# Moving tiles of the matmul pairs at one common word offset, 512 words apart, in a fused attention and relu² kernel

## The chip, the cores and the metric

The kernel runs on one core of one Trainium2 chip. The metric is the device time of one execution in microseconds (us). TensorE is called PE below, its weight loads PEld, VectorE DVE, ScalarE ACT, GpSimd POOL, and SyncE, which issues the transfers, SP. Memory on the core is counted in words of 4 bytes along one partition, and "phase" is used in this document for the first word of an operand modulo 64 words.

## The reference

Four batches of 12,480 tokens with 128 channels attend through 32 inducing points, and the result passes through a feed-forward layer with 2,048 hidden units, squared relu and an affine step.

```python
def mab(q, kv):
    s = scale * (q @ kv.transpose(0, 2, 1))
    s = s - s.max(-1, keepdims=True)
    a = np.exp(s)
    a /= a.sum(-1, keepdims=True) + 1e-09
    return a @ kv
h = mab(I, x)
x = mab(x, h)          # (B, N, C), then reshaped to (B * N, C)

h = x @ w_in
r = np.maximum(h, 0.0)
g = s * (r * r) + b
return (g @ w_out).astype(np.float32)
```

Inputs and output are float32; the two feed-forward weights come as 64-bit floats and are narrowed on the chip.

## The kernel before, in words

Tokens are worked on in 104 blocks of 480 (`BLK`), 26 for each batch. A block has 8 pairs (`NPAIR`), each of two chunks of 128 hidden units. For a pair, `pair` at L839 issues two matmuls at L850: weights from `wst` (the batch's inducing points already multiplied with `w_in`, in two float32r parts), moving operand the block's attention weights `a2t`, 128 partitions by 480 words. The result `h` goes through relu (`r`, on ACT at L865 or DVE at L867) and is squared twice: rounded to float32r as `g1` on ACT (`square`, L933), and in full as `g` on DVE (L888). Then `g2 = g - g1`, the small remainder, is made at L910, on POOL for 670 pairs and on DVE for 156. Finally `out_part` multiplies at L958 with w_out, six matmuls for each pair: `w_lo` and `w_hi` with both chunks of `g1`, and `w_hi` with both chunks of `g2`. So a pair costs eight float32r matmuls of 480 columns: two at L850, six at L958. The first six pairs (`NATIVE`) do without the remainder and multiply `g` in plain float32 with w_out.

Where these moving operands lie: `g1` is a tile of four chunks for two pairs (4 buffers), `g2` of two chunks for one pair (8 buffers), with chunks 480 words apart, and `a2t` one chunk (3 buffers, used in turn by the blocks). In the layout of the built program all `g1` and `g2` tiles begin at phase 48, so, since 480 is seven and a half times 64, their chunks alternate between phase 48 and 16. The three `a2t` buffers begin at phases 32, 0 and 32; blocks 2, 5, 8 and so on, counted from 0, have the one at phase 0. The weights `w_hi` and `w_lo` lie at phase 16, `wst` at phase 0.

The order on every engine is settled before the program is built: `Plan.run` simulates all engines with fixed durations (for example `MM` = 0.2174 us for each matmul), and the instructions are recorded in the order of that simulation. Each engine then runs its own list in order; semaphores hold it where an operand isn't ready. Before the first pair there is an opening of some 46 us in which batch 0's inducing points are computed (`p1_unit`, L429, `h_out`, L549, `attend_first`, L766), with the loads of x as the main traffic. The other batches' scores, values and attention weights (`scores`, `values`, `attend`) are spread between the pairs.

Small tiles that the change touches: `e` (the exponentials of the opening, two buffers, L459), the opening's `acc` (L434), `identr` (a float32r identity, used once at L804), and `t4` (a sum of parts of the identity, L229).

Of the kernel before, what the change touches and what calls it, by code (L numbers as in the profile page):

```python
# [10 lines left out]
F32 = mybir.dt.float32  # L11
F32R = mybir.dt.float32r
# [7 lines left out]
P = 128  # L20
T = 120
NQ = 4
BLK = T * NQ
# [40 lines left out]
    ("x", 5), ("w_in", 3), ("x", 6), ("w_out", 1), ("q", 5), ("w_out", 2), ("w_out", 3),  # L64
)
WARM = 6

# [84 lines left out]
def tile_attn_relu2(ctx: ExitStack, tc: tile.TileContext, xT, xN, xQ, indT, w_in, w_out, s_rep, b_rep, outT):  # L154
    nc = tc.nc
    B, _, N = xT.shape
    M = indT.shape[1]
# [5 lines left out]
    NG = -(-NBLK // GR)  # L163
# [3 lines left out]
    const = ctx.enter_context(tc.tile_pool(name="const", bufs=1))  # L167
    xt_pool = ctx.enter_context(tc.tile_pool(name="xt", bufs=XT))
    xn_pool = ctx.enter_context(tc.tile_pool(name="xn", bufs=4))
    p1 = ctx.enter_context(tc.tile_pool(name="p1", bufs=1))  # L170
    p2 = ctx.enter_context(tc.tile_pool(name="p2", bufs=2))
    wst_pool = ctx.enter_context(tc.tile_pool(name="wst", bufs=2))
    sm = ctx.enter_context(tc.tile_pool(name="sm", bufs=2))
    ew = ctx.enter_context(tc.tile_pool(name="ew", bufs=1))
# [37 lines left out]
    ind_sb = const.tile([P, M], F32, name="ind_sb")  # L212
    s_sb = const.tile([P, 1], F32, name="s_sb")
    b_sb = const.tile([P, 1], F32, name="b_sb")
    w_in_sb = const.tile([P, F], F32, name="w_in_sb")
    w_hi = const.tile([P, NF, P], F32R, name="w_hi")
    w_lo = const.tile([P, NF, P], F32R, name="w_lo")
    bias = const.tile([P, 1], F32, name="bias")
    ident = const.tile([P, P], F32, name="ident")
    make_identity(nc, ident)  # L220
    identr = const.tile([P, P], F32R, name="identr")
    nc.vector.tensor_copy(out=identr, in_=ident)
    ones = const.tile([P, M], F32, name="ones")
    nc.vector.memset(ones, 1.0)
# [1 line left out]
    nc.vector.memset(rebias, -896 * 2.0**23)  # L226

    sel = const.tile([P, P], F32, name="sel")
    t4 = sm.tile([P, 2, M], F32, name="t4", bufs=1)  # L229
    idv = ident.rearrange("p (r i) -> p r i", i=M)  # L230
    nc.vector.tensor_add(out=t4, in0=idv[:, 0:2, :], in1=idv[:, 2:4, :])
    nc.vector.tensor_add(
# [5 lines left out]
    def blocks_in(g):  # L238
        return min(GR, NBLK - g * GR)
# [188 lines left out]

    def p1_unit(g, ps, *waits):  # L429
        if not st:  # L430
            d = st[0] = {
                "mx": sm.tile([P, NG], F32, name="mx"),
                "l": sm.tile([P, NG], F32, name="l"),
                "acc": p1.tile([P, NG, P], F32, name="s"),  # L434
            }
            last = M * blocks_in(NG - 1)
            if last < P:
                nc.vector.memset(d["mx"][last:P, NG - 1:NG], -3.0e38)
                nc.vector.memset(d["l"][last:P, NG - 1:NG], 0.0)
                nc.vector.memset(d["acc"][last:P, NG - 1, :], 0.0)  # L440
        d = st[0]
        nb = blocks_in(g)
        rows = M * nb
        yield "PE", 0.98, ("x", 0, g, 1), *waits
        ps = ps()
        xt = xt_tiles[0, g, 1][0]
        for q in range(nb):
            nc.tensor.matmul(ps[M * q:M * (q + 1), 0:BLK], ind_sb, xt[:, q], start=True, stop=True)
        x_used(g, "s")
        yield "DVE", 0.69  # L450
        mx = d["mx"][0:rows, g:g + 1]
        nc.vector.reduce_max(out=mx, in_=ps[0:rows, 0:BLK], axis=AX.X)  # L452
        plan.set(("top", 0, g))
        yield "DVE", 0.08
        nm = sm.tile([P, 1], F32, name="nm")[0:rows]
        nc.vector.tensor_scalar_mul(nm, mx, -scale)
        e_turn, e_free = ring_in_order("e", 2)
        yield "ACT", 0.75, *e_free
        e = sm.tile([P, BLK], F32, name="e", bufs=2)  # L459
        plan.set(("e", "got", e_turn))  # L460
        nc.scalar.activation(
            out=e[0:rows], in_=ps[0:rows, 0:BLK], func=AF.Exp, bias=nm, scale=scale,
            accum_out=d["l"][0:rows, g:g + 1],
        )
        plan.set(("e", 0, g))
        yield "PE", 0.45
        for q in range(NQ):
            nc.tensor.transpose(ps[0:T, q * P:q * P + rows], e[0:rows, q * T:(q + 1) * T], ident[0:rows, 0:rows])
        plan.set(("e", e_turn))
        e_turn, e_free = ring_in_order("eT", 3)  # L470
        yield dict(ACT=0.49, DVE=0.61), 0.0, *e_free
        eT = sm.tile([T, NQ, P], F32, name="eT", bufs=3)
        plan.set(("eT", "got", e_turn))
        copy(eT[:, :, 0:rows], ps[0:T].rearrange("p (q i) -> p q i", q=NQ)[:, :, 0:rows])
        js = [g * GR // SB + h for h in range(-(-nb // SB))]
        yield "PE", 0.2 + 0.21 * nb, *[("turn", j) for j in js]
        for q in range(NQ):
            for n in range(nb):
                nc.tensor.matmul(  # L479
                    ps[M * n:M * (n + 1), 0:P], eT[:, q, M * n:M * (n + 1)],  # L480
                    home["xn"][js[n // SB] % 4][:, n % SB, q, :], start=(q == 0), stop=(q == NQ - 1),
                )
        plan.set(("eT", e_turn))
        for j in js:
            plan.set(("v done", j))
            if j >= NSB - 4:
                plan.set(("xn", j % 4))
        yield dict(ACT=0.18, DVE=0.21), 0.0
        copy(d["acc"][0:rows, g, :], ps[0:rows, 0:P])
        plan.set(("p1", 0, g))  # L490
# [227 lines left out]
    a2t, halves = {}, {}  # L718
# [47 lines left out]
    def attend_first(ps):  # L766

        yield "PE", 0.8, ("hT", 0), ("x", 0, 0, 2)
        ps = ps()
        xt = xt_tiles[0, 0, 2][0]  # L770
        for q in range(NQ):
            nc.tensor.matmul(
                ps[0:T, M * q:M * (q + 1)], xt[:, 0, q * T:(q + 1) * T], st[0]["hT"][:, 0:M], start=True, stop=True
            )
        v = ps[0:T, 0:P].rearrange("p (n i) -> p n i", i=M)
        sums = ps[0:T, P:P + NQ]
        yield "DVE", 0.28
        mx = sm.tile([P, TB], F32, name="mx2")[0:T, 0:NQ]
        nc.vector.reduce_max(out=mx, in_=v, axis=AX.X)
        yield "DVE", 0.28  # L780
        nc.vector.tensor_tensor(out=v, in0=v, in1=mx.unsqueeze(2).broadcast_to([T, NQ, M]), op=ALU.subtract)
        yield "ACT", 0.28
        nc.scalar.activation(out=v, in_=v, func=AF.Exp, scale=scale)
        yield "DVE", 0.28
        nc.vector.reduce_sum(out=sums, in_=v, axis=AX.X)
        yield "DVE", 0.16
        nc.vector.tensor_scalar_add(sums, sums, 1e-9)
        yield "DVE", 0.18
        l = sm.tile([P, TB], F32, name="l2")[0:T, 0:NQ]
        nc.vector.reciprocal(out=l, in_=sums)  # L790
        yield "DVE", 0.28
        nc.vector.tensor_tensor(out=v, in0=v, in1=l.unsqueeze(2).broadcast_to([T, NQ, M]), op=ALU.mult)
        yield dict(ACT=0.38, DVE=0.43), 0.0
        A = p2.tile([P, 2, WC], F32R, name="hl")
        A = A.rearrange("p a t -> p (a t)")[0:T, 0:NQ * P].rearrange("p (n r s i) -> p n r s i", n=NQ, r=2, s=2)
        vr = v.unsqueeze(2).broadcast_to([T, NQ, 2, M])
        copy(A[:, :, :, 0, :], vr)
        yield "DVE", 0.43
        nc.vector.tensor_tensor(out=A[:, :, :, 1, :], in0=vr, in1=A[:, :, :, 0, :].bitcast(F32), op=ALU.subtract)
        n, free = ring_in_order("a2t", 3)  # L800
        yield "PE", 0.5
        for q in range(NQ):
            w = A[:, q].rearrange("p r s i -> p (r s i)")
            nc.tensor.transpose(ps[:, q * T:(q + 1) * T].bitcast(F32R), w, identr[0:T, 0:T])  # L804
        yield dict(ACT=0.57, DVE=0.66), 0.0, *free
        t = p2.tile([P, BLK], F32R, name="a2t", bufs=3)
        plan.set(("a2t", "got", n))
        copy(t, ps[:, 0:BLK])
        a2t[0, 0] = t, n
        plan.set(("a2t", 0, 0))  # L810
        plan.set("first")

    def spread(b, g, q):

        turn, free = ring_in_order("a2t", 3)
        yield "SP", 2.4 if b or g else 1.6, *free, ("hl", b, g)
        t = p2.tile([P, BLK], F32R, name="a2t", bufs=3)
        plan.set(("a2t", "got", turn))
        hl, n, left = halves[b, g]
        for r in range(P // M):  # L820
            nc.sync.dma_start(
                out=t[M * r:M * (r + 1)].bitcast(F32), in_=hl[M * q:M * (q + 1), r % 2].bitcast(F32)
            )
        left.remove(q)
        if not left:
            plan.set(("hl", n))
        a2t[b, GR * g + q] = t, turn
        plan.events["a2t", b, GR * g + q] = landing(0.7) if b or g else landing(0.3, 1.7)
# [10 lines left out]
    def pair(k):  # L839

        b, blk, pr = place(k)
        n = pr % 2
# [5 lines left out]
        for u in range(2):  # L848
            c = 2 * pr + u
# [8 lines left out]
        q = quad[k - n]  # L858
# [4 lines left out]
        r = q["r_t"][:, half, :]  # L863
# [22 lines left out]
        g = hv if kind == "D" else ew.tile([P, 2, BLK], F32, name="g", bufs=4)  # L886
# [18 lines left out]
        n2, free2 = ring("g2", 8)  # L905
        yield ("Pool", 2.237, ("Q", k), free2) if kind == "P" else ("DVE", 1.065, C_U, ("Q", k), free2)
        hi = q["g1_t"][:, half, :]
        g2 = ew.tile([P, 2, BLK], F32R, name="g2", bufs=8)
        eng = nc.gpsimd if kind == "P" else nc.vector
        eng.tensor_tensor(out=g2, in0=g, in1=hi.bitcast(F32), op=ALU.subtract)  # L910
        plan.set(("h", turn) if kind == "D" else ("g", g_turn))
# [9 lines left out]
    def square(k0):  # L921

        q = quad[k0]
# [4 lines left out]
        if hi - lo == 2:  # L928
            plan.extend(0.8)
        if "g1_t" not in q:  # L930
            q["g1_t"] = ew.tile([P, 4, BLK], F32R, name="g1", bufs=4)
        sl = slice(2 * lo, 2 * hi)
        nc.scalar.activation(out=q["g1_t"][:, sl, :], in_=q["r_t"][:, sl, :], func=AF.Square)  # L933
        for i in range(lo, hi):
# [210 lines left out]
```

## Time and profile before

| | us |
|---|---|
| median of 3 runs | 1600.81 (1600.46 to 1603.71) |
| the profiled execution, device time | 1600.12 |
| its span from first to last instruction | 1598.0 |
| share of the span in which the chain that ended last stood on PE | 97% |

Durations of a trace come from the profiled execution, so sums are made against its 1598.0 us, and 2.1 us lie around the span. A matmul's end in the trace is modelled, and matmuls overlap in it: the distance from one start to the next, called the step below, is what a matmul costs. A row such as `x3304 | 1072.8, 380` gives the count, the busy time of all together, and the mean duration of one in ns.

### The profile page before, as it was taken

How to read it: one execution, taken by the hardware profiler on the slowest of the kernel's cores; microseconds unless marked ns; L12 is line 12 of the kernel's file. 1: busy time of each engine (PE TensorE's matmuls, PEld its weight loads, DVE VectorE, ACT ScalarE, POOL GpSimd, SP SyncE). 2: the span in 40 equal slices, each digit the busy share in tenths (PEclk: the TensorE clock that was granted, in tenths of full speed). 3: DMA queues.
4: the chain of work that ended last, by engine and by line, in shares of the span. 5: the costliest groups of instructions: out<-in, count | busy, mean ns of one | idle time of the engine just before them, and what ended most of it. 6: DMA issues, size and time to landing. Idle time of an engine off the chain costs nothing.

```text
span 1598.0 us, 24588 instructions
## 1 busy us (share of the span) xinstructions
PE 1584.9 (99%) x8155; PEld 1290.3 (81%) x8155; DVE 1485.2 (93%) x1603; ACT 1477.3 (92%) x1703; POOL 1499.6 (94%) x677
## 2 busy tenths in 40 slices
PE   8999999999999999999999999999999999999999
PEld 5578788888888778888788778888888888888887
DVE  6999899999999999999999899999999999999997
ACT  7799999999999989999999998999999999999997
POOL 0399999999999999999999999999999999999998
PEclk9999999999999999999999999999999999999999
DMA  8422323212223323211222322322221112112100
GB/s 292 125 92 89 128 77 107 81 32 89 75 75 112 99 100 112 84 59 57 82 68 88 118 76 91 120 79 63 84 56 61 38 50 69 32 50 69 57 27 24
DMA packets 54251, 131.17 MB, mean 82 GB/s; under 512 B 11518, under 2 KB 38014, under 8 KB 54126
## 3 DMA queue, kind: packets, MB, share of 16 engines
q1 hardware_dynamic: 54126, 129.61, 25.4%
q8 instruction: 66, 1.08, 0.3%
q14 instruction: 59, 0.48, 0.1%
HBM read 74.50 MB, written 25.56 MB: 63 GB/s over the span
## 4 chain that ended last, share of the span: by engine, by line
PE 97%; DMA 2%; DVE 1%; SPq 0%; ACT 0%; issue 0%; DVEq 0%; ACTq 0%
PE x L958 68%; PE h L850 24%; PE x L728 2%; PE x L676 1%; PE x L631 1%; DMA g<-in_w_in_dram 1%; DMA xn<-in_xQ_dram 0%; DMA xt<-in_xT_dram 0%; SPq L599 0%; PE x L581 0%; PE h L479 0%; DMA wst<-hl 0%; ACT xn L185 0%; DVE mx L452 0%; DVE wst L319 0%
## 5 line engine op out<-in xcount | busy, mean ns | idle before, releaser
L910 POOL TENSOR_TENSOR g<-g,g 128x960 fp32r<-128x960 f32 x670 | 1498.4, 2284 | 92.0 <-DVE g L888 75.4
L958 PE MATMUL x<-g,w_hi 128*128 128x480 f32 x3304 | 1072.8, 380 | 0.0
L933 ACT ACTIVATE g<-r 128x960 fp32r<-128x960 f32 (+1 forms) x766 | 803.5, 1072 | 33.7 <-DVE r L867 15.9
L888 DVE SCALAR_TENSOR_TENSOR g<-h,r 128x960 f32<-128x960 f32 x670 | 756.2, 1148 | 32.5 <-ACT r L865 23.1
L958 PEld LDWEIGHTS x<-g,w_hi 128*128 128x128 f32 x3304 | 620.3, 188 | 102.4 <-issue 3.9
L865 ACT ACTIVATE r<-h 128x960 f32<-128x960 f32 x639 | 613.2, 969 | 53.1 <-PE h L850 41.9
L958 PE MATMUL x<-g,w_lo 128*128 128x480 f32 x1652 | 628.0, 380 | 0.0
L850 PE MATMUL h<-a2t,wst 128*128 128x480 f32 x1664 | 510.3, 388 | 3.1 <-DMA wst<-hl 2.8
L850 PEld LDWEIGHTS h<-a2t,wst 128*128 128x128 f32 x1664 | 299.4, 188 | 103.0 <-issue 39.9
L958 PEld LDWEIGHTS x<-g,w_lo 128*128 128x128 f32 x1652 | 309.9, 188 | 52.2 <-issue 2.4
L867 DVE TENSOR_SCALAR r<-h 128x960 f32<-128x960 f32 x193 | 222.6, 1153 | 23.8 <-PE h L850 17.7
L888 DVE SCALAR_TENSOR_TENSOR h<-h,r 128x960 f32<-128x960 f32 x156 | 180.2, 1158 | 6.7 <-ACT r L865 6.1
L910 DVE TENSOR_TENSOR g<-h,g 128x960 fp32r<-128x960 f32 x156 | 179.2, 1151 | 4.7
L966 ACT ACTIVATE ob<-x,bias,s_sb 128x480 f32<-128x480 f32 x103 | 77.4, 752 | 12.8 <-PE x L958 12.3
L728 PE MATMUL x<-xt,hT 128*32 128x480 f32 x208 | 28.3, 578 | 0.0
L759 DVE TENSOR_TENSOR hl<-x,hl 128x480 fp32r<-128x480 f32 (+1 forms) x28 | 18.4, 657 | 9.8 <-ACT hl L185 9.7
L631 PE MATMUL x<-xt,ind_sb 128*32 128x480 f32 x156 | 21.2, 578 | 0.0
L734 DVE STREAM_TRANSPOSE x<-x 128x480 f32<-128x480 f32 (+1 forms) x28 | 19.3, 688 | 1.6 <-PE x L728 1.6
L676 PEld LDWEIGHTS x<-xn,eT 128*32 128x32 f32 (+1 forms) x630 | 17.5, 109 | 4.0 <-issue 2.7
L676 PE MATMUL x<-xn,eT 128*32 128x128 f32 (+1 forms) x630 | 20.7, 274 | 0.0
L752 DVE STREAM_TRANSPOSE x<-x 128x480 f32<-128x480 f32 (+1 forms) x28 | 19.5, 697 | 0.9
L750 DVE TENSOR_TENSOR x<-x,l 128x480 f32<-128x480 f32 (+1 forms) x28 | 18.6, 665 | 0.9
(148 smaller groups left out, 363.2 us busy)
## 6 DMA issues: line engine op xcount, KB each, us to landing
xt<-in_xT_dram SPq DMA_DIRECT2D x41, 960.0 KB, 5.3
out_dram<-ob SPq DMA_DIRECT2D x104, 240.0 KB, 2.0
a2t<-hl SPq DMA_DIRECT2D x412, 60.0 KB, 2.0
xn<-in_xN_dram SPq DMA_DIRECT2D x18, 512.0 KB, 4.6
xn<-in_xN_dram SPq DMA_DIRECT2D x18, 448.0 KB, 5.6
xt<-in_xT_dram SPq DMA_DIRECT2D x13, 480.0 KB, 4.1
wst<-hl SPq DMA_DIRECT2D x64, 64.0 KB, 2.0
r<-in_xT_dram SPq DMA_DIRECT2D x7, 480.0 KB, 9.2
```

The costliest lines, as they stand in the source:

```text
L631: nc.tensor.matmul(ps[M * q:M * (q + 1), 0:BLK], ind_sb, xt[:, q], start=True, stop=True)
L676: nc.tensor.matmul(ps[M * c:M * (c + 1), 0:P], eT[0:rows, n], xn_tiles[b, g, half][0][0:rows, n - half * TH], start=m < P // M, stop=m + P ...
L728: nc.tensor.matmul(ps[M * q:M * (q + 1), 0:BLK], hT[:, 0:M], xt[:, q], start=True, stop=True)
L752: nc.vector.transpose(out=s, in_=s)
L850: nc.tensor.matmul(h[:, u, 0:BLK], wst[:, c * P:(c + 1) * P], A, start=True, stop=True)
L865: nc.scalar.activation(out=r, in_=hv, func=AF.Relu)
L867: nc.vector.tensor_scalar(out=r, in0=hv, scalar1=0.0, scalar2=None, op0=ALU.max)
L888: nc.vector.scalar_tensor_tensor(out=g, in0=hv, scalar=0.0, in1=r, op0=ALU.max, op1=ALU.mult)
L910: eng.tensor_tensor(out=g2, in0=g, in1=hi.bitcast(F32), op=ALU.subtract)
L933: nc.scalar.activation(out=q["g1_t"][:, sl, :], in_=q["r_t"][:, sl, :], func=AF.Square)
L958: nc.tensor.matmul(o, w, g, start=first and n == 0, stop=left == 0 and n == len(ops) - 1)
L966: nc.scalar.activation(out=ob, in_=o, func=AF.Identity, bias=bias, scale=s_sb)
```

## The change

Five things change:

- `g1` and `g2` are allocated with 512 words for each chunk (`RUN`), and the chunk is words 3 to 482 of it (`G_OFF`). `a2t` gets 512 words too, and its operand is words 19 to 498 (`A_OFF`).
- A tile `pad` of 32 words is allocated ahead of the small tiles and cleared on POOL. With it all `g1` and `g2` tiles again begin at phase 48, and all `a2t` tiles at phase 32; so each chunk of all three begins at phase 51. `w_hi` and `w_lo` stay at phase 16, `wst` comes to lie at phase 32.
- To make room, the opening's `e` and `acc` become slices of one tile in the place of the later batches' scores `s`; `identr` takes the place of the later `accb`, and `t4` that of `s2`.
- Engine instructions that read or write `g1` or `g2` as 960 words in one run now go over two runs of 480.
- Matmuls, weights, the planner's numbers and the order are the same.

```diff
+RUN = 512
+A_OFF = 19
+G_OFF = 3
...
+    pad = sm.tile([P, 32], F32, name="pad", bufs=1)
+    nc.gpsimd.memset(pad, 0.0)
...
-    identr = const.tile([P, P], F32R, name="identr")
+    identr = sm.tile([P, P], F32R, name="accb", bufs=1)
...
-    t4 = sm.tile([P, 2, M], F32, name="t4", bufs=1)
+    t4 = p2.tile([P, P], F32, name="s2", bufs=1)[:, 0:2 * M].rearrange("p (r i) -> p r i", i=M)
...
     def p1_unit(g, ps, *waits):
         if not st:
+            room = p1.tile([P, NG * BLK], F32, name="s")
...
-                "acc": p1.tile([P, NG, P], F32, name="s"),
+                "acc": room[:, 0:NG * P].rearrange("p (g c) -> p g c", g=NG),
+                "e": [room[:, NG * P + n * BLK:NG * P + (n + 1) * BLK] for n in range(2)],
...
-        e = sm.tile([P, BLK], F32, name="e", bufs=2)
+        e = d["e"][e_turn % 2]
...
-        t = p2.tile([P, BLK], F32R, name="a2t", bufs=3)
+        t = p2.tile([P, RUN], F32R, name="a2t", bufs=3)[:, A_OFF:A_OFF + BLK]
...
-        g2 = ew.tile([P, 2, BLK], F32R, name="g2", bufs=8)
+        g2 = ew.tile([P, 2, RUN], F32R, name="g2", bufs=8)[:, :, G_OFF:G_OFF + BLK]
...
-            q["g1_t"] = ew.tile([P, 4, BLK], F32R, name="g1", bufs=4)
+            q["g1_t"] = ew.tile([P, 4, RUN], F32R, name="g1", bufs=4)[:, :, G_OFF:G_OFF + BLK]
```

The `a2t` line stands twice in the kernel (L806 and L817) and changes alike in both.

On POOL the list before begins like this; `g_113` is the tile for PE's warm-up matmuls, and the first remainders (L910) follow:

```order
L1141 UNCONDITIONAL_BRANCH
masks.py:197 MEMSET ident 128x128
L1070 MEMSET g_113 128x512
masks.py:199 ISA
masks.py:199 AFFINE_SELECT ident<-ident 128x128
L910 TENSOR_TENSOR g_780<-g,g_765 128x960
L910 TENSOR_TENSOR g_810<-g,g_798 128x960
```

In the changed program (line numbers there are 7 higher, 910 is 917) the same place reads:

```order
L1148 UNCONDITIONAL_BRANCH
L219 MEMSET pad 128x32
masks.py:197 MEMSET ident 128x128
L1077 MEMSET g_115 128x512
masks.py:199 ISA
masks.py:199 AFFINE_SELECT ident<-ident 128x128
L917 TENSOR_TENSOR g_775<-g,g_760 128x2x480
```

One small clearing comes first, and each remainder goes over two runs of 480 in place of one of 960; nothing else moves on POOL.

On ACT, in the middle of the program (relu at L865 and squares at L933 between an output at L966 and a later batch's exponentials at L661), the list before is:

```order
L865 ACTIVATE r<-h 128x960
L933 ACTIVATE g_7393<-r 128x960
L185 CAST hl<-x_86 128x480
L933 ACTIVATE g_7429<-r 128x960
L865 ACTIVATE r<-h 128x960 x2
L966 ACTIVATE ob<-x_85,bias,s_sb 128x480
```

and in the changed program:

```order
L872 ACTIVATE r<-h 128x960
L940 ACTIVATE g_7388<-r 128x2x480
L188 CAST hl<-x_86 128x480
L940 ACTIVATE g_7424<-r 128x2x480
L872 ACTIVATE r<-h 128x960 x2
L973 ACTIVATE ob<-x_85,bias,s_sb 128x480
```

The order is the same, and only the squares' shape differs. On PE, DVE and SP no instruction changes its place either.

More of the change, by code (lines that the diff above doesn't have):

```diff
@@ L816, in spread @@
         yield "SP", 2.4 if b or g else 1.6, *free, ("hl", b, g)
-        t = p2.tile([P, BLK], F32R, name="a2t", bufs=3)
+        t = p2.tile([P, RUN], F32R, name="a2t", bufs=3)[:, A_OFF:A_OFF + BLK]
         plan.set(("a2t", "got", turn))
```

## The prediction

> **What bounds the kernel now.** First the page's head: busy time by engine, the granted clock in 40 slices, and the chain that ended last.
>
> ```profile
> span 1598.0 us, 24588 instructions
> ...
> PE 1584.9 (99%) x8155; PEld 1290.3 (81%) x8155; DVE 1485.2 (93%) x1603; ACT 1477.3 (92%) x1703; POOL 1499.6 (94%) x677
> ...
> PEclk9999999999999999999999999999999999999999
> ...
> PE 97%; DMA 2%; DVE 1%; SPq 0%; ACT 0%; issue 0%; DVEq 0%; ACTq 0%
> PE x L958 68%; PE h L850 24%; PE x L728 2%; PE x L676 1%; PE x L631 1%; DMA g<-in_w_in_dram 1%; DMA xn<-in_xQ_dram 0%; DMA xt<-in_xT_dram 0%; SPq L599 0%; PE x L581 0%; PE h L479 0%; DMA wst<-hl 0%; ACT xn L185 0%; DVE mx L452 0%; DVE wst L319 0%
> ```
>
> PE ends the kernel: 97% of the chain is on it, 92% on the two lines whose operands the change moves, at full clock throughout. So the question is what one of these matmuls costs. The groups of instructions give their number (3304 + 1652 + 1664 = 6,620) and modelled durations.
>
> ```profile
> L910 POOL TENSOR_TENSOR g<-g,g 128x960 fp32r<-128x960 f32 x670 | 1498.4, 2284 | 92.0 <-DVE g L888 75.4
> L958 PE MATMUL x<-g,w_hi 128*128 128x480 f32 x3304 | 1072.8, 380 | 0.0
> ...
> L958 PE MATMUL x<-g,w_lo 128*128 128x480 f32 x1652 | 628.0, 380 | 0.0
> ...
> L850 PE MATMUL h<-a2t,wst 128*128 128x480 f32 x1664 | 510.3, 388 | 3.1 <-DMA wst<-hl 2.8
> ```
>
> The step, from start to start, is read from the timeline of PE alone (start, length of the merged row, count).
>
> ```profile
> 799.87 0.38 PE L958 MATMUL x<-g,w_lo 128*128 128x480 f32 x1
> 800.08 0.38 PE L958 MATMUL x<-g,w_hi 128*128 128x480 f32 x1
> 800.30 0.38 PE L958 MATMUL x<-g,w_lo 128*128 128x480 f32 x1
> 800.52 0.81 PE L958 MATMUL x<-g,w_hi 128*128 128x480 f32 x3
> 801.17 0.59 PE L850 MATMUL h<-a2t,wst 128*128 128x480 f32 x2
> ...
> 802.25 0.81 PE L958 MATMUL x<-g,w_hi 128*128 128x480 f32 x3
> 802.90 0.38 PE L958 MATMUL x<-g,w_lo 128*128 128x480 f32 x1
> ```
>
> From 799.87 to 802.90 there are 14 steps: 0.216 us each. Three in one row last 0.81, one 0.38, so two steps are 0.43: a duration is the step plus about 162 ns. A mean of 380 is then a step of 218 ns, and 6,620 steps are 1,443 of the 1,598 us. Minimum, median and maximum of the durations show that the step isn't one number.
>
> ```profile
> L958 PE MATMUL x<-g,w_hi x3304: 372/381/487, 65.2 to 1593.7; 128*128 128x480 f32 x195
> ...
> L958 PE MATMUL x<-g,w_lo x1652: 372/382/484, 65.0 to 1593.0; 128*128 128x480 f32 x184
> ```
>
> 372 means 210 ns, 382 means 220 ns: work of one shape at one clock differs by 5%, and no wait is named in front of it (idle 0.0 above). The nearest view that sets addresses apart takes line 850 by blocks: blocks 26 and 32 have the `a2t` buffer at phase 0, blocks 27 and 33 one at phase 32, block 44 again phase 0.
>
> ```profile
> L850 PE MATMUL h<-a2t,wst x16: 375/377/442, 435.5 to 447.9; 128*128 128x480 f32 x16
> L850 PE MATMUL h<-a2t,wst x16: 372/381/459, 449.8 to 461.9; 128*128 128x480 f32 x16
> L850 PE MATMUL h<-a2t,wst x16: 375/377/394, 524.3 to 535.3; 128*128 128x480 f32 x16
> L850 PE MATMUL h<-a2t,wst x16: 373/381/483, 536.4 to 553.8; 128*128 128x480 f32 x16
> L850 PE MATMUL h<-a2t,wst x17: 375/381/454, 703.7 to 716.4; 128*128 128x480 f32 x17
> ```
>
> Two pairs of neighbours say that phase 0 is 4 ns cheaper (medians 377 against 381); the last row, phase 0 at 381, says that the phase alone doesn't settle it. What was read just before, at which phase, can matter as well. The only run of matmuls with one operand address throughout is in the warm-up, four of 480 columns at phase 48; three of them:
>
> ```profile
> L1078 PE MATMUL h<-g x3: 374/374/382, 42.5 to 42.9; 128*128 128x480 f32 x3
> ```
>
> Their mean is 377, a step of 215, at the phase where the mixed sequence has its medians of 381 and 382.
>
> **The change, part by part.**
>
> *The moving operands.* All 6,620 steps get phase 51 before and after them. Phases 0, 16, 32 and 48 are in the trace, 51 is not, so the value has to be bounded: below by the fastest step, 372 (210 ns, 8 less than the mean, 53 us in all), above by the slow level, 382 (220 ns, 2 more, 13 us). I take 214 ns, between the fast level of the phase 0 blocks (375 to 377, so 213 to 215) and the warm-up's 215, since a sequence of one phase is what the change makes. Some 80 steps end at other work, so 6,540 × 4 ns = 26 us come off PE's path: 1598.0 - 26 = 1572.
>
> *What is late next.* POOL. Its first and last remainders, from its timeline, and its group between 100 and 1500 us:
>
> ```profile
> 62.48 2.23 POOL L910 TENSOR_TENSOR g<-g,g 128x960 fp32r<-128x960 f32 x1 [60.75 <-DVE g L888]
> ...
> 1583.13 9.00 POOL L910 TENSOR_TENSOR g<-g,g 128x960 fp32r<-128x960 f32 x4
> ...
> L910 POOL TENSOR_TENSOR g<-g,g 128x960 fp32r<-128x960 f32 x615 | 1375.4, 2284 | 26.8 <-ACT g L933 12.6 <-DVE g L888 11.4 <-DVE x L745 1.3
> ```
>
> Of 1,400 us it is idle for 27. It starts at 62.48, has 1498.4 us of work, and 5.9 us of the span follow its end at 1592.13: 62.5 + 1498.4 + 5.9 = 1566.8 us is a floor under the span, whatever the matmuls cost. So at most 31 us can be gained. With PE's own path at 1572, 5 us above that floor, both would be busy nearly throughout, and a late remainder now stalls PE. For that I add 6 us, a fifth of POOL's 31 us of slack, between 0 and the 15 us of half of it: 1578, and with 2.1 us around the span **1580**.
>
> *Two runs in place of one* on POOL (670), DVE (156) and ACT (706 squares of one pair, 60 of two). No row has POOL over two runs. DVE's two forms of L888 differ in just that, and in where they write:
>
> ```profile
> L888 DVE SCALAR_TENSOR_TENSOR g<-h,r 128x960 f32<-128x960 f32 x670 | 756.2, 1148 | 32.5 <-ACT r L865 23.1 <-POOL g L910 2.3 <-issue 0.5
> ...
> L888 DVE SCALAR_TENSOR_TENSOR h<-h,r 128x960 f32<-128x960 f32 x156 | 180.2, 1158 | 6.7 <-ACT r L865 6.1
> ```
>
> 10 ns more. By that POOL would gain 670 × 10 = 7 us of work, and the floor rises to 1574; below, an odd word could also change nothing or save as little, so -7 to +7 us for POOL. ACT's 766 squares and DVE's 156 get under 8 and 2 us at that price, where these engines stand idle for 121 and 113 us of the span. I take 0, as the reading and writing itself is the same 960 words, and keep the 7 us in the range.
>
> *Transfers into `a2t`.* 412 issues land in 2.0 us (median), as the page's transfer part has it, into a ring of three buffers for blocks of some 15 us. Where that cover goes, a block waits as long as its transfer is late; between 0 and 1 us more for each transfer, nothing reaches the pairs. I take 0.
>
> ```profile
> a2t<-hl SPq DMA_DIRECT2D x412, 60.0 KB, 2.0
> ```
>
> *The opening.* `e`, `acc`, `t4` and `identr` keep their engines, order and waits; only places change, and the later owners (`s`, `s2`, `accb`) come after their last use. The `pad` clearing stands ahead of the two on which PE's first warm-up waits:
>
> ```profile
> 0.73 0.21 POOL masks.py:197 MEMSET ident<- 128x128 f32 x1 [0.29 <-POOLq L1135]
> 0.87 0.53 POOL L1070 MEMSET g<- 128x512 f32 x1
> ...
> 4.61 1.66 PE L423 MATMUL h<-ident,xt 128*120 128x128 f32 x8 [0.33 <-DMA xt<-in_xT_dram]
> ```
>
> It has a quarter of `ident`'s words, so it costs at most its 0.21 us, and PE waits for x at 4.61 anyway: 0, with 0.2 as the other end.
>
> **Rivals.**
>
> *Nothing happens (1600).* A step may depend on other things than the operand's start: block 44 above has phase 0 and the slow median. Phase 51 may also lie among the others, as a mean of 218. Then the step stays, PE stays the bound, and the time is 1600 within 3 us. Against it: 377 to 381 in neighbouring blocks. In a sentence by itself: the Trainium skill's page "SBUF — State Buffer", section "Who interferes with whom", gives PE read ports of its own and says that PE never waits on anyone, by which the place of its operand would matter to nobody; the trace, with 372 to 382 for one shape, agrees only as far as no wait is named.
>
> *The slow level everywhere (slower).* One phase for all can as well fix each step at the upper level: 382, of which the warm-up row has one. The place is PE at L850 and L958, the price 6,540 × 2 ns = 13 us, so 1613; it decides as soon as phase 51 costs more than today's mean of 218 ns. What speaks for it: 48 is the nearest phase in the trace, and the groups that begin there have 381 and 382 as medians. A rule of the Trainium skill bears on this (page "SBUF — State Buffer", "Specifications (TRN2)"): memory lines are 16 bytes, and each crossing to a new one pays. Word 51 isn't a multiple of four words, so 480 words from there touch 121 lines where they touched 120; as an estimate by that rule a step grows by 218 / 120 = 1.8 ns, 12 us in all, 1612. No row before has an operand off a line's start, so the trace can't yet say.
>
> *POOL slower (slower).* Two runs from an odd word on POOL, all 670 times: with 31 us of slack it decides from 31 / 670 = 47 ns an instruction (2%). At 100 ns the floor is 1566.8 + 67 + 2.1 = 1636. Against it: 10 ns is the only such difference that a row shows.
>
> **How the numbers follow.** The forecast (PE's steps fall, POOL holds the rest) gets 0.60: 1569, floor and 2.1 us, to 1592, where POOL's 7 us and half its slack are lost. Nothing happens: 0.15, 1597 to 1604. Slow level: 0.15, 1612 to 1616. POOL slower: 0.10, 1605 to 1640. The predicted time is 1580, 1.3% under the profiled execution's 1600.12, which stands 0.7 us from the median of the runs. The range from 1567 to 1612 holds the first two cases and the nearest edge of the others, some 0.8. A measurement of this kernel tells 0.2% (3 us) from no change: faster 0.61, same 0.13, slower 0.26.
>
> **What would show it.** After the change the medians of L850 and L958 should fall from 381 and 382 to 374 to 378, with minimum and median closer together; POOL's idle time after its first remainder should shrink from 31 us to about 15, and waits of PE for POOL's L910 should appear, where no row above has one. POOL's mean should stay at 2284; 2330 or more would make it the bound and the forecast wrong. Medians at 382 or above with POOL unchanged would be the slow level, medians where they are the first rival. A step far under 210 would be a gain that I don't foresee, and POOL's floor would then show as PE waiting.

## The result, and the profile after

| | before | after |
|---|---|---|
| median, us | 1601.74 (1600.46 to 1603.71, 4 runs) | 1584.19 (1583.92 to 1584.55, 4 runs) |
| ratio to before | | 0.989 (95% interval 0.9872 to 0.9907) |
| span of the profiled execution, us | 1598.0 | 1582.0 |

The kernel became 1.1% faster. First the head of the page after: busy times, the chain that ended last, and the costliest groups. Line numbers are 7 higher than before (850 is 857, 958 is 965).

```profile
span 1582.0 us, 24589 instructions
...
PE 1567.9 (99%) x8155; PEld 1285.4 (81%) x8155; DVE 1481.6 (94%) x1603; ACT 1472.2 (93%) x1703; POOL 1499.3 (95%) x678
...
PE 93%; DVE 2%; ACT 1%; issue 1%; POOL 1%; DMA 1%; SPq 0%; DVEq 0%; ACTq 0%; POOLq 0%
...
L917 POOL TENSOR_TENSOR g<-g,g 128x960 fp32r<-128x960 f32 x670 | 1498.1, 2296 | 77.2 <-DVE g L895 71.3
L965 PE MATMUL x<-g,w_hi 128*128 128x480 f32 x3304 | 1058.1, 375 | 0.0
...
L965 PE MATMUL x<-g,w_lo 128*128 128x480 f32 x1652 | 619.2, 375 | 0.0
L857 PE MATMUL h<-a2t,wst 128*128 128x480 f32 x1664 | 506.7, 385 | 4.3 <-DMA wst<-hl 2.9
```

The mean on the w_out line fell from 380 to 375 with nothing else on PE changed. PE's share of the chain fell from 97% to 93%; DVE has 2% in place of 1%, and ACT and POOL have 1% each. The views of those two lines (minimum, median and maximum duration in ns, of all matmuls) show what became of the spread:

```profile
L965 PE MATMUL x<-g,w_hi x3304: 374/375/485, 67.1 to 1577.7; 128*128 128x480 f32 x195
...
L965 PE MATMUL x<-g,w_lo x1652: 374/375/485, 66.9 to 1577.1; 128*128 128x480 f32 x184
...
L857 PE MATMUL h<-a2t,wst x1664: 374/375/758, 46.9 to 1570.0; 128*128 128x480 f32 x185
```

Before, the first two read 372/381 and 372/382, and the `a2t` line read:

```profile
L850 PE MATMUL h<-a2t,wst x1664: 372/381/756, 46.6 to 1585.9; 128*128 128x480 f32 x185
```

The minimum has risen by 2 ns, and the median has come down to within 1 ns of it: a step is now 213 or 214 ns nearly always. Taken from the starts of consecutive matmuls of the two lines (6,540 steps), the mean of those under 226 ns fell from 217.6 to 213.5. The view of waits gives for both kernels those in front of PE's weight loads, where a pair that waits for its buffer `h` shows. Before:

```profile
PEld h L850 <- issue: 39.9, 112, 1.9
...
PEld h L850 <- DVE g L888: 8.2, 12, 0.8
```

and after (us in total, times, longest):

```profile
PEld h L857 <- issue: 44.1, 117, 1.9
PEld h L857 <- DVE g L895: 14.5, 33, 0.8
```

Waits for DVE's squaring (L895, which reads `h`) went from 12 to 33, by 6.3 us, and those for which the profile names nothing ("issue") grew by 4.2 us. That is where most of the missing part of the gain went, as the account of PE's time up to the start of the last of these matmuls (1593.7 and 1577.7 us) shows:

| us | before | after | difference |
|---|---|---|---|
| 6,540 steps at the mean of those under 226 ns | 1423.1 | 1396.3 | -26.8 |
| the rest of the later ones (221, then 283) | 21.1 | 30.3 | +9.2 |
| other work between the blocks | 102.9 | 104.1 | +1.2 |
| start of the first pair | 46.6 | 46.9 | +0.4 |
| together | | | -16.0 |

The 1.2 us of the third row are the clock's and not the change's. In the changed kernel's profiled execution the granted clock was half for 3.4 us of the work ahead of the first w_out matmuls (0.50 between 52 and 54 us), where the kernel before had it in full, and from the first `a2t` matmul to the first w_out matmul it took 20.0 us in place of 18.4. In the traces below that keep this order, that stretch takes 18.4 us where the clock was full (phases 52, 56 and 59 among them), 19.9 to 20.1 where it was half for 3.4 us, and 21.3 in the one where it was half for 6.8 us (phase 50). Between the later matmuls, on which the mean steps rest, the clock was full in all of them.

### The profile page after: what moved, and what is told of

Its sections match the earlier page's. It is cut to its first block, busy times and chain, and to the rows that moved or that the text cites. A ratio compares the mean times of both kernels' runs of the same rounds, so it can differ in the third digit from the quotient of the medians.

```text
span 1582.0 us, 24589 instructions
## 1 busy us (share of the span) xinstructions
PE 1567.9 (99%) x8155; PEld 1285.4 (81%) x8155; DVE 1481.6 (94%) x1603; ACT 1472.2 (93%) x1703; POOL 1499.3 (95%) x678
## 4 chain that ended last, share of the span: by engine, by line
PE 93%; DVE 2%; ACT 1%; issue 1%; POOL 1%; DMA 1%; SPq 0%; DVEq 0%; ACTq 0%; POOLq 0%
PE x L965 64%; PE h L857 23%; PE x L735 2%; PE x L638 1%; POOL g L917 1%; PE x L683 1%; DVE g L895 1%; ACT g L940 1%; DVE r L874 1%; PE h L428 1%; DMA xn<-in_xQ_dram 0%; ACT r L872 0%; SPq L606 0%; DVE h L895 0%; DVE g L917 0%
## 5 line engine op out<-in xcount | busy, mean ns | idle before, releaser
L917 POOL TENSOR_TENSOR g<-g,g 128x960 fp32r<-128x960 f32 x670 | 1498.1, 2296 | 77.2 <-DVE g L895 71.3
L965 PE MATMUL x<-g,w_hi 128*128 128x480 f32 x3304 | 1058.1, 375 | 0.0
L895 DVE SCALAR_TENSOR_TENSOR g<-h,r 128x960 f32<-128x960 f32 x670 | 755.8, 1148 | 29.4 <-ACT r L872 22.6
L965 PE MATMUL x<-g,w_lo 128*128 128x480 f32 x1652 | 619.2, 375 | 0.0
L857 PE MATMUL h<-a2t,wst 128*128 128x480 f32 x1664 | 506.7, 385 | 4.3 <-DMA wst<-hl 2.9
L857 PEld LDWEIGHTS h<-a2t,wst 128*128 128x128 f32 x1664 | 296.3, 188 | 110.2 <-issue 44.1
L895 DVE SCALAR_TENSOR_TENSOR h<-h,r 128x960 f32<-128x960 f32 x156 | 180.2, 1158 | 6.0 <-ACT r L872 5.5
L917 DVE TENSOR_TENSOR g<-h,g 128x960 fp32r<-128x960 f32 x156 | 179.2, 1151 | 4.7
L766 DVE TENSOR_TENSOR hl<-x,hl 128x480 fp32r<-128x480 f32 (+1 forms) x28 | 18.4, 657 | 8.8 <-ACT hl L188 8.6
```

The source lines that it names most:

```text
L857: nc.tensor.matmul(h[:, u, 0:BLK], wst[:, c * P:(c + 1) * P], A, start=True, stop=True)
L895: nc.vector.scalar_tensor_tensor(out=g, in0=hv, scalar=0.0, in1=r, op0=ALU.max, op1=ALU.mult)
L965: nc.tensor.matmul(o, w, g, start=first and n == 0, stop=left == 0 and n == len(ops) - 1)
```

## The experiments

Mean steps below are those of steps under 226 ns, "late" the time by which the others exceed the median, in sum (20.8 us before, 30.5 after; the table above counts from the mean). Each kernel of this section ran once, except the two of the planner at its end; seven runs of the kernel before on one chip lie between 1599.85 and 1602.66 us, so a difference in time of less than 3 us says nothing by itself. The first question: is it one phase for all, or phase 51?

**Phase 48 for all, and phase 0 for all.**

```diff
-A_OFF = 19
-G_OFF = 3
+A_OFF = 16     # and 32 in the second run
+G_OFF = 0      # and 16 in the second run
```

> All moving tiles of the pairs begin at phase 48 in place of 51, still one phase for all and 512 words apart; nothing else differs from the changed kernel. Theory A (one phase for all is what counts, whichever it is): median durations of the two matmul lines stay at 375 (step 213), time 1584 within 3 us. Theory B (the phase itself has a price, and one phase for all fixes every step at that phase's price): the groups that began at phase 48 before had medians of 381 and 382, so step 219 to 220 and time 1600 to 1616. Rule of the memory lines of 16 bytes: 48 is a multiple of four words, 51 is not, so the step would fall by 1.8 ns to about 212, and POOL would hold the time at 1575 to 1584. POOL's mean: 2284 if 51 being odd made it 2296, 2296 if the two runs of 480 did.

> All moving tiles at phase 0. Theory A: step 213, 1584 within 3 us. Theory B: the price of phase 0 in the kernel before was lowest (377 in the blocks with that buffer, step 215), so step 213 to 216 and 1584 to 1594. Rule of the memory lines: 212, as at any multiple of four words.

Phase 48 took 1603.71 us, beside 1600.34 before on the same chip; mean step 218.0. Phase 0 took 1596.35; mean step 216.4. Here is the row of `w_hi` at phase 48, whose median at 51 is 375:

```profile
L965 PE MATMUL x<-g,w_hi x3304: 373/381/488, 67.5 to 1597.3; 128*128 128x480 f32 x195
```

Theory A is out. Both kernels have all else of the change (one phase for all, 512 words between chunks, the new places of the small tiles and of `wst`), and it brings nothing at 48 and 1.2 of the 4 ns at phase 0. The phase itself has a price. It isn't quite the price that theory B read off the kernel before: that gave 219 to 220 at 48 and 213 to 216 at 0.

**Phases 52 and 56, then 50 and 59**, by the same two numbers (4 and 20, 8 and 24, 2 and 18, 11 and 27).

> All moving tiles at phase 52, one word on from 51 and the next multiple of four. If the memory lines of 16 bytes set the price, 52 is better than 51: step 212 to 213. If the price changes slowly with the phase: 213 to 214, 1582 to 1587. If 51 is good because it is odd: step 216 to 218 as at phases 0 and 48, 1596 to 1603.

> All moving tiles at phase 56, half way between 48 (step 218.0) and 0 (216.4). If only multiples of 16 words are dear: 213 to 214, 1582 to 1587. If 51 is a narrow optimum: 215 to 218, 1590 to 1603.

> All moving tiles at phase 50, one word ahead of 51; 52, one word behind it, had a step of 218.5, most of them at 220. If 51 is the last good phase before an edge at 52: 213 to 214 here too, 1582 to 1587. If 51 is a well one word wide: 216 to 219, 1596 to 1604.

> All moving tiles at phase 59, eight words on from 51. The steps of the kernel before lie 3.3 ns apart (210, 213, 217, 220), which is the time of eight columns at 480 columns in 200 ns; if the price of a phase repeats with eight words, 59 locks at 213 as 51 does: 1582 to 1587. If it repeats with 16, 32 or 64 words or not at all: 215 to 220, 1590 to 1605, as at 56 (217.4).

| phase of all moving tiles | 48 | 50 | 51 | 52 | 56 | 59 | 0 |
|---|---|---|---|---|---|---|---|
| mean step, ns | 218.0 | 219.3 | 213.5 | 218.5 | 217.4 | 214.7 | 216.4 |
| time, us | 1603.71 | 1611.38 | 1584.19 | 1604.51 | 1599.24 | 1587.36 | 1596.35 |

The view of the w_lo matmuls at 50, 52 and 59, in this order, one row of each kernel:

```profile
L965 PE MATMUL x<-g,w_lo x1652: 376/382/488, 68.2 to 1604.3; 128*128 128x480 f32 x184
```

```profile
L965 PE MATMUL x<-g,w_lo x1652: 376/381/487, 65.2 to 1597.5; 128*128 128x480 f32 x184
```

```profile
L965 PE MATMUL x<-g,w_lo x1652: 374/374/479, 65.7 to 1580.3; 128*128 128x480 f32 x184
```

A word to either side of 51 costs 5 to 6 ns a step. At 52, 4,032 of the 6,340 undisturbed steps are 220 ns; at 51, 5,996 of 6,257 are 213 or 214. Eight words on, at 59, the w_out line has a median of 374 again (mean step 214.4), and the steps of the a2t line are dearer (mean 215.8). So the price looks as if it came back after eight words, though 48 and 56 (218.0, 217.4) and 0 (216.4) differ by up to 1.6 ns; two cheap places don't settle a period. Another reading fits the seven kernels as well: the two cheap phases, 51 and 59, are the odd ones, and the five dear ones are even. No third odd phase was tried, so whether 51 is cheap as an odd start or as one narrow place stays open. What 52 rules out is a price that is low at multiples of four words or that changes slowly with the phase, and 56 rules out that only multiples of 16 words are dear. At 50 step and time lie above every expectation; of the time some 3 us are the opening's clock, by the account above, and not the step.

**Only g1 and g2 moved.** `a2t` as before the change, `pad` made 128 words so that `a2t` and `wst` lie at their phases from before (32, 0, 32 and 0), and `g1` and `g2` as in the change; the `a2t` line stands twice and changes alike in both places:

```diff
-    pad = sm.tile([P, 32], F32, name="pad", bufs=1)
+    pad = sm.tile([P, 128], F32, name="pad", bufs=1)
-        t = p2.tile([P, RUN], F32R, name="a2t", bufs=3)[:, A_OFF:A_OFF + BLK]
+        t = p2.tile([P, BLK], F32R, name="a2t", bufs=3)
```

> g1 and g2 at phase 51, 512 apart, as in the change; a2t and wst as before the change (a2t at phases 32, 0, 32, wst at 0). Theory A (what precedes matters): steps inside L958's sequences fall to 213, but those at and around L850 keep a spread up to 220, as each pair changes phase twice; mean of the line that works on g1 and g2 214 to 216, of the other 216 to 219; 1586 to 1592. Theory B (each operand's own price): line of g1 and g2 at 213.5 throughout, the a2t line at 217 to 219 as before: 1,664 x 4.2 = 7 us of the 26 lost, 1586 to 1590. They differ in the spread of the steps just after an a2t matmul: 210 to 220 by A, 213 to 214 by B.

1589.47 us: the `a2t` part of the change, with the move of `wst` from phase 0 to 32 that comes with it, is worth 5 us. The a2t line's mean step is 217.1, the w_out line's 214.8. The first step on g1 or g2 after an a2t matmul has a mean of 217.5 (10th to 90th percentile 214 to 223), the second 216.4, the next eight 213.3 to 214.4; in the changed kernel the first two are 213.5 and 213.4. Both theories have a share: the phase has its price, and a2t matmuls as they were before disturb the next two steps. Whether that is their moving operand's phase or that of `wst`, this run doesn't tell apart.

**Weights at another phase.** `w_hi` and `w_lo` at phase 48:

```diff
-    pad = sm.tile([P, 32], F32, name="pad", bufs=1)
+    pad = sm.tile([P, 64], F32, name="pad", bufs=1)
...
+    pad2 = const.tile([P, 32], F32, name="pad2")
+    nc.gpsimd.memset(pad2, 0.0)
     w_hi = const.tile([P, NF, P], F32R, name="w_hi")
     w_lo = const.tile([P, NF, P], F32R, name="w_lo")
+    pad3 = const.tile([P, 32], F32, name="pad3")
+    nc.gpsimd.memset(pad3, 0.0)
...
-        sw = sm.tile([P, NG, M], F32, name="sw", bufs=1)
+        sw = d["room"][:, NG * P + 2 * BLK:NG * P + 2 * BLK + NG * M].rearrange("p (g m) -> p g m", g=NG)
```

> The changed kernel with w_hi and w_lo at phase 48 in place of 16 (a pad of 32 words ahead of them and one behind; the opening's sw becomes a slice of the same tile as e); the moving tiles stay at phase 51, wst at 32. If the price depends on the distance from the weights that are loaded meanwhile: that distance falls from 35 to 3 words, near the 0 of the pairs 16 on 16 before the change (217), so the step on the w_out line rises to 215 to 218 while the a2t line stays at 213 to 214 where another a2t matmul follows: 1588 to 1600. If the moving operand's phase alone counts: 213.5 on both, 1584 within 3 us.

1589.25 us; mean steps 214.8 on both lines. Sorted by the matmul that comes next, the steps tell more: where it is an a2t matmul, whose weights didn't move, they have a mean of 213.7 on both lines (213.7 and 213.8 in the changed kernel), and where it multiplies with `w_hi` or `w_lo` they have 214.4 to 215.9 (213.3 to 213.9). So the place of the weights of the next matmul matters too, by 1 to 2.4 ns. That the moving operand's phase alone counts is out. The theory of the distance was right about where the step rises, with a size at or under the lower edge of the 215 to 218 ns that it gave; one other place of the weights doesn't show that the distance is what counts.

**What gave 10 us back: POOL or DVE?** POOL makes half of each remainder (edits on the path of the 670 pairs alone):

```diff
-        eng.tensor_tensor(out=g2, in0=g, in1=hi.bitcast(F32), op=ALU.subtract)
+        c = slice(0 if kind == "D" else 1, 2)
+        eng.tensor_tensor(out=g2[:, c], in0=g[:, c], in1=hi[:, c].bitcast(F32), op=ALU.subtract)
...
+        ops = [(w_hi[:, 2 * pr + u, :], g2[:, u if kind == "D" else 1, :]) for u in range(2)]
```

> The changed kernel, but POOL makes the remainder of the second chunk alone (480 of 960 words), and that chunk's matmul operand is used for both chunks; the first chunk's remainder is left out, on the 670 pairs that POOL has. PE's work is the same. If POOL is what gave back 10 of the 26 us: late steps (over 226 ns) fall back to 20 us or under, time 1570 to 1576. If the late steps come from DVE and ACT (buffers of h that come free late): they stay near 30 us and the time at 1581 to 1585.

POOL's group, and then PE's waits, in that kernel:

```profile
L918 POOL TENSOR_TENSOR g<-g,g 128x480 fp32r<-128x480 f32 x670 | 818.3, 1232 | 753.9 <-ACT g L941 358.9 <-DVE g L895 292.6 <-DVE x L752 26.2
```

```profile
PEld h L857 <- issue: 43.9, 116, 1.9
PEld h L857 <- DVE g L895: 14.6, 33, 0.8
```

POOL now stands idle for 754 us, PE's waits are what they were (33 for DVE), late steps are 30.6 us, and the time is 1584.33. POOL, 99% busy from its first remainder to its last in the changed kernel, costs that kernel nothing. Then DVE's half as well:

```diff
-            nc.vector.scalar_tensor_tensor(out=g, in0=hv, scalar=0.0, in1=r, op0=ALU.max, op1=ALU.mult)
+            c = slice(0 if kind == "D" else 1, 2)
+            nc.vector.scalar_tensor_tensor(
+                out=g[:, c], in0=hv[:, c], scalar=0.0, in1=r[:, c], op0=ALU.max, op1=ALU.mult
+            )
```

> As the run with POOL's half, and in addition DVE makes g for the second chunk alone on those 670 pairs (480 of 960 words), so that h is free some 0.5 us earlier; the first chunk's square is left out too. PE's work is the same. If late buffers of h behind DVE are what gave back 10 of the 26 us: late steps fall from 30 us to 21 or under, time 1570 to 1576. If the rest is PE's own (the fixed 85 ns at pairs with an extra semaphore instruction, other work between): late steps stay at 28 to 31, 1581 to 1585.

What the idle time ahead of L857 waited for in that kernel, from the view of that line (us, times):

```profile
  issue: 34.2, 68
...
  DVE g L896: 1.6, 2
```

1569.44 us, late steps 17.8 us (133 of them), the step unchanged at 213.4, and 2 waits for DVE's squaring (L896 there) in place of 33. So what holds the pairs back is `h`, which DVE frees late. The run doesn't tell apart whether that is DVE's whole load or the length of this one instruction. Nor does it show that a shorter squaring would give the whole kernel these 15 us: POOL's half is left out here too, and with whole remainders POOL's floor of 1566.8 us would lie right at this kernel's span of 1567.3.

**The order laid out for the new step.** One planner number (the edit below), and then eight more settings, which the second expectation lists (`R_LEAN` has two numbers):

```diff
-MM = 0.2174
+MM = 0.2135
```

> The changed kernel with one number of the planner changed: a matmul counts 0.2135 us in place of 0.2174, so that the order on all engines is laid out for the step that the chip now has. If the 10 us were given back since DVE's steps stand in an order made for slower matmuls, pairs wait less for h: late steps 20 to 26 us, time 1574 to 1581. If DVE's work is simply too much: late steps stay at 30, time 1581 to 1587.

> As the run before, with seven more of the planner's numbers moved (R_LEAN -0.237 and 0.006, M_U -6.98, R_U 2.287, SQ 3.166, S_U -0.7626, C_U -7.1767, POOL_Q 3.0111, OUT 1.9883), picked from 55 random settings as the shortest plan. If order is what holds the pairs back: late steps under 24 us and 1570 to 1578, faster than the changed kernel by 0.4 to 0.9%. If not: 1581 to 1587.

The first gave 1585.72 us (1584.89 to 1587.03; ratio to before 0.9901, 0.9884 to 0.9917) with late steps of 33 us: no gain; waits for POOL came in the place of some for DVE.

```profile
PEld h L857 <- DVE g L895: 12.6, 23, 0.9
PEld x L965 <- POOL g L917: 11.1, 22, 1.3
```

The second gave 1581.30 (1580.42 to 1583.27; ratio 0.9876, 0.9861 to 0.989), the lowest of the kernels that leave nothing out; late steps 27.2 us. It is 4 us under the first on the same chip (in the profiled executions 1.6 us of that are the opening's clock, half for 3.4 us in the first and full in the second), but its interval overlaps that of the changed kernel (0.9872 to 0.9907), so that it beats it isn't shown. The expectation of 1570 to 1578 was missed. Nor is it the order alone that these two plans change: POOL makes 667 and 663 of the remainders in them, in place of 670, and DVE the rest.

## Why the prediction came out, step by step

- *PE bounds the kernel, so the step is what counts.* Right; 26.8 us came off PE's undisturbed steps, where 26 were forecast.
- *The step: 214 ns, from the fast blocks and the warm-up.* Right in size (213.5). The reason behind it was wrong: I took a sequence of one phase to be what makes a step cheap, and one phase for all at 48, 50 or 52 has 218 to 219. The rows that I took 213 to 215 from were at phases 0 and 48, and with these phases for all the step is 216.4 and 218.0. That 51 is cheap could not be read from the trace of before, which has no phase that isn't a multiple of 16; the value was a choice between bounds that happened to be met, which is luck. The runs show a price of the phase itself, which differs by 5 to 6 ns from one word to the next.
- *What is late next: POOL, with a floor at 1566.8 us of span.* This is the step that failed. POOL's busy share was read as a floor, and 6 us were added for PE waiting on it. One sign of it came out, as POOL's idle time after its first remainder fell from 31.2 to 14.5 us; the other didn't, as PE waits for POOL's remainders once, 0.4 us, after the change and once, 0.3 us, before. Halving POOL's work changed nothing, halving DVE's squaring too took the span to 1567.3. The next bound is `h`, three buffers that DVE frees. The size, 9.2 us for the 6 that I put, was near by chance. The floor itself held: the changed kernel lies 15 us above it. In sum 16.0 us came off the span, where 20 were forecast.
- *Two runs in place of one.* ACT (1009 before, 1010 after on squares of one pair) and DVE (1151 both times) show no cost. POOL's mean rose by 12 ns, but its busy union stayed (1498.4 and 1498.1), and kernels with two runs at other phases lie between 2279 and 2294: no cost shown.
- *Opening and transfers.* The first pair starts 0.4 us later, against 0 to 0.2 (in the other kernels of phase alone it starts between 46.7 and 47.3 us, so one trace doesn't show this to be the change's); `a2t` still lands in 2.0 us.
- *The rival of the memory lines* (the Trainium skill's page "SBUF — State Buffer", "Specifications (TRN2)") doesn't set the step here: 52, a multiple of four words, is 5 ns dearer than 51. The rule by which PE never waits on anyone (the Trainium skill's page "SBUF — State Buffer", "Who interferes with whom") names no reason for a step of 213 or 219 by one word; the runs can't say whether, or on what, the matmul waits there.
- *The slow level for all* was a real rival: it is what 52 and 50 do, at 1604.51 and 1611.38.

What stays open is the mechanism: the price depends on the moving operand's phase, on the phase of the next matmul's weights and on the matmuls just ahead, and the runs don't say why.

## What to carry to other kernels

When one instruction of one shape has a spread of durations with no wait named, look at where its operands lie: here 5 ns of 218 hung on one word of offset, and neighbours one word away were as dear as the start. Such an offset is found by trying several, odd ones among them, not by aligning. And before a nearly full engine is called the next bound, look at whom the waiting engine waits for: POOL at 99% cost nothing, while a buffer that DVE frees cost most of 9 us.

## What the runs showed of the hardware that I had not expected

At phase 50 POOL's remainder takes 1891 ns in place of 2296 (each of the 670 between 1879 and 1917), the same 960 words from and to the same tiles, two words off where `g` begins (phase 48):

```profile
L917 POOL TENSOR_TENSOR g<-g,g 128x960 fp32r<-128x960 f32 x670 | 1251.4, 1891 | 348.9 <-DVE g L895 158.8 <-ACT g L940 147.1 <-DVE x L752 16.8
```

At 48, 51, 52, 56, 59 and 0 it is 2279 to 2296. One run doesn't say whether the distance of two words or phase 50 itself is what counts. That kernel was the slowest of all, as its steps were 219 ns. A kernel with its matmul operands at 51 and `g` moved to 49, to keep two words of distance, and with more pairs on POOL, was not tried.
